# The first chunk's h in two 256-row halves, w1 in 256-column pieces, and a warm-up of 32-column tiles

## The chip, the cores and the metric

The kernel runs on one core of one Trainium2 chip. The metric is device time in microseconds (us). Every timed execution quoted here is fast, with a granted TensorE clock of 0.999 to 1.0. The profile of a kernel is one execution, and its span is about 1.8 us shorter than its device time. PE is TensorE, DVE VectorE, ACT ScalarE, SPq the queue of transfers that SyncE issues.

## The reference

A dense layer with SiLU, forward and backward, in bfloat16: x is 2048 x 640, w1 640 x 1536, w2 1536 x 640. The kernel returns the output and the three gradients.

```python
h = silu(einsum("bsd,df->bsf", x, w1))
out = einsum("bsf,fd->bsd", h, w2)
# returned: out, and the gradients of x, w1 and w2 for a given grad_out
```

## The kernel before

It works in four chunks of 512 rows. For a chunk it makes h transposed (w1's columns on the partitions), then the out phase (h times w2). The first chunk decides the ramp: it needs x transposed (xT), which PE makes from x in its natural layout, and w1. Warm-up matmuls on zeros keep PE busy until x is there.

```python
NWARM = 36
warm = cpool.tile([P, P], dt_in, name="warm")
nc.vector.memset(warm[:], 0.0)
for i in range(NWARM):
    nc.tensor.matmul(wp[:, 0:P], lhsT=warm[:], rhs=warm[:], start=True, stop=True)
# ... (cut)
nc.sync.dma_start(out=x_nat[:, 0:STC, :], in_=x_v[:, 0:STC, :])          # 512 rows, 640 KB
nc.sync.dma_start(out=w1_nat[:, :, 0:FH], in_=w1_v[:, :, 0:FH])          # 256 columns, 320 KB
nc.sync.dma_start(out=w1_nat[:, :, FH:FC], in_=w1_v[:, :, FH:FC])        # 320 KB
for fc in range(1, NFC):                                                 # 2 x 640 KB
    nc.sync.dma_start(out=w1_nat[:, :, fc * FC:(fc + 1) * FC], in_=...)
for hf in range(2):                                                      # w2, halves of its columns
    nc.sync.dma_start(out=w2_nat[:, :, hf * DH:(hf + 1) * DH], in_=...)
goT_next = load_goT(0)                                                   # a transposing load
# ... (cut: transposing loads of w2 and w1)
xT_next = pe_xT(0, 1)                     # 20 PE transposes, copies by DVE and ACT

def h_group(ft, xT, aT, ghT):             # 128 columns of h: 5 matmuls of 512 columns
    hp = ps_h.tile([P, SC], FP32, name="hp")
    for dt_ in range(DT):
        nc.tensor.matmul(hp[:], lhsT=w1_nat[:, dt_, ft * P:(ft + 1) * P], rhs=xT[:, dt_, :], ...)
    # ... (cut: SiLU and its derivative on ACT and DVE)

def sd_phase(...):                        # the out phase
    for ft in range(FT):
        for hf in range(2):               # the second matmul already reads w2's second half of columns
            nc.tensor.matmul(op_[:, hf, 0:DH], lhsT=lhs_all[:, ft, ...],
                             rhs=rhs_all[:, ft, hf * DH:(hf + 1) * DH], ...)
```

## Time and profile before

| | before |
|---|---|
| device time, median of 3 | 323.03 us (323.01 to 323.51) |
| span of the profile | 321.2 us |
| x landed, first h matmul | 5.01 us, 6.35 us |
| first out-phase matmul | 19.30 us |
| the two parts of w2 landed | 14.79 us and 18.60 us |

The head of the page: busy time of PE, and its digits over 40 slices of 8 us.

```profile
PE 316.2 (98%) x1926; PEld 188.5 (59%) x1944; DVE 99.1 (31%) x172; ACT 78.9 (25%) x136; POOL 0.7 (0%) x6
...
PE   8999999999999999999999999999999999999996
...
PEclk9999999999999999999999999999999999999999
...
PE 97%; DMA 1%; issue 0%; DVE 0%; DVEq 0%
```

PE is never idle for long after the first slice, and the chain of waits that ended last (the last line) is PE itself. So the kernel can only get shorter where PE has nothing to do, at the start. The table of PE's waits shows all there is:

```profile
PE wp L90 <- DVE warm L85: 1.0, 1, 1.0
PE tp L118 <- DMA x_nat<-in_x_dram: 0.3, 1, 0.3
```

The timeline of PE, first 20 us (start, duration, line, operation; in brackets the idle time before and what ended it):

```profile
0.99 3.81 PE L90 MATMUL wp<-warm 128*128 128x128 bf16 x36 [0.99 <-DVE warm L85]
5.06 1.30 PE L118 MATMUL tp<-ident,x_nat 128*128 128x128 bf16 x20 [0.26 <-DMA x_nat<-in_x_dram]
6.35 13.11 PE L144 MATMUL hp<-xT,w_nat 128*128 128x512 bf16 x58
19.30 0.98 PE L180 MATMUL op<-w_nat,aT 128*128 128x320 bf16 x6
```

The warm-up covers the wait for x. Its matmuls start 107 ns apart up to 4.38 us and 56 ns apart from 4.47: the array's clock opens there. The page's row PEclk does not show this, it has 9 throughout. x lands, is transposed, and from 6.35 us PE works through. (Two of the 60 h matmuls have no record.) The same start in the chain of waits:

```profile
0.74 4.26 DMA x_nat<-in_x_dram
5.01 0.05 issue
5.06 1.30 PE tp L118 x20
6.35 0.37 PE hp L144
```

### The profile page before, as it was taken

The page shows a single profiled execution, that of the slowest core. Times are in us where ns is not written, and L with a number is a line of the kernel's source. Part 1 is how long each engine was busy: PE and PEld are TensorE (multiplying, and loading weights), DVE is VectorE, ACT ScalarE, POOL GpSimd, SP SyncE. Part 2 cuts the span into 40 slices and gives each one's busy share as a digit, 9 for nine tenths or more (in the row PEclk, how much of TensorE's full clock was granted, in tenths as well). Part 3 has the DMA queues.
Part 4 walks back from the last instruction along what each step waited for, and adds up shares of the span by engine and source line. Part 5 has one row for each costly group of instructions (what it writes and reads, how often), then busy time and mean ns, then how long its engine had stood idle before and what let it go on. Part 6 is the DMA issues. An engine that isn't in the chain of part 4 may idle for free.

```text
span 321.2 us, 4386 instructions
## 1 busy us (share of the span) xinstructions
PE 316.2 (98%) x1926; PEld 188.5 (59%) x1944; DVE 99.1 (31%) x172; ACT 78.9 (25%) x136; POOL 0.7 (0%) x6
## 2 busy tenths in 40 slices
PE   8999999999999999999999999999999999999996
PEld 6467457544577644477754467777777775444443
DVE  1860553577501287800357740220000000110001
ACT  3961000455210155411044521001111111000100
POOL 0000000000000000000000000000000000000000
PEclk9999999999999999999999999999999999999999
DMA  7999999998794020291020079909999996211111
GB/s 235 318 191 200 220 274 241 363 289 274 213 290 137 6 78 0 78 316 67 17 82 0 0 254 245 239 17 236 226 218 213 266 219 211 85 38 44 35 42 41
DMA packets 113731, 52.32 MB, mean 163 GB/s; under 512 B 84144, under 2 KB 113712, under 8 KB 113712
## 3 DMA queue, kind: packets, MB, share of 16 engines
q1 hardware_dynamic: 113712, 52.04, 64.1%
q8 instruction: 15, 0.25, 0.3%
q14 instruction: 4, 0.03, 0.0%
HBM read 9.18 MB, written 21.76 MB: 96 GB/s over the span
## 4 chain that ended last, share of the span: by engine, by line
PE 97%; DMA 1%; issue 0%; DVE 0%; DVEq 0%
PE op L180 32%; PE op L263 16%; PE hp L163 16%; PE hp L144 16%; PE hp L302 15%; DMA x_nat<-in_x_dram 1%; PE hp L284 1%; PE tp L118 0%; DVE g_2755 L295 0%; DVEq L295 0%
## 5 line engine op out<-in xcount | busy, mean ns | idle before, releaser
L144 PE MATMUL hp<-xT,w_nat 128*128 128x512 bf16 x229 | 56.3, 379 | 0.6
L163 PE MATMUL hp<-goT,w2T 128*128 128x512 bf16 x238 | 56.8, 379 | 0.1
L180 PE MATMUL op<-w1T,ghT 128*128 128x320 bf16 x384 | 52.8, 299 | 0.0
L180 PE MATMUL op<-w_nat,aT 128*128 128x320 bf16 x384 | 52.8, 299 | 0.0
L263 PE MATMUL op<-go_nat,a_blk 128*128 128x320 bf16 x384 | 52.3, 299 | 0.0
L151 ACT ACTIVATE aT<-hp 128x512 bf16<-128x512 f32 x48 | 28.7, 597 | 83.0 <-PE hp L144 83.0
L302 PE MATMUL hp<-gh_blk,x_nat 128*128 128x512 bf16 x219 | 48.2, 379 | 0.3
L180 PEld LDWEIGHTS <-aT 128*128 128x128 bf16 x384 | 37.5, 98 | 15.3
L180 PEld LDWEIGHTS <-ghT 128*128 128x128 bf16 x384 | 37.5, 98 | 14.8
L263 PEld LDWEIGHTS <-a_blk 128*128 128x128 bf16 x384 | 37.5, 98 | 14.7
L163 PEld LDWEIGHTS <-w2T 128*128 128x128 bf16 x240 | 23.5, 98 | 28.2
L144 PEld LDWEIGHTS <-w_nat 128*128 128x128 bf16 x240 | 23.4, 98 | 27.8
L170 DVE SCALAR_TENSOR_TENSOR ghT<-ghT,hp 128x512 bf16<-128x512 bf16 x48 | 32.5, 682 | 16.2 <-PE hp L163 16.2
L191 DVE CAST o_sb<-op 128x640 bf16<-128x640 f32 x16 | 13.2, 825 | 78.6 <-PE op L180 78.6
L302 PEld LDWEIGHTS <-x_nat 128*128 128x128 bf16 x224 | 21.9, 98 | 26.3
L156 DVE SCALAR_TENSOR_TENSOR ghT<-aT,v 128x512 bf16<-128x512 bf16 x48 | 33.0, 687 | 0.6
L153 ACT ACTIVATE t<-hp 128x512 f32<-128x512 f32 x48 | 28.4, 592 | 0.0
L155 DVE TENSOR_SCALAR v<-t 128x512 bf16<-128x512 f32 x48 | 20.5, 427 | 20.5 <-ACT t L153 20.5
L189 ACT ACTIVATE o_sb<-op 128x640 bf16<-128x640 f32 x16 | 11.2, 703 | 49.1 <-PE op L180 49.1
L270 ACT ACTIVATE gw_sb<-op 128x640 bf16<-128x640 f32 x12 | 8.4, 704 | 56.8 <-PE op L263 56.8
L313 DVE CAST g_2475<-hp 128x512 bf16<-128x512 f32 x1 | 0.7, 690 | 58.2 <-PE hp L302 58.2
L90 PE MATMUL wp<-warm 128*128 128x128 bf16 x36 | 3.8, 304 | 1.0 <-DVE warm L85 1.0
(31 smaller groups left out, 26.2 us busy)
## 6 DMA issues: line engine op xcount, KB each, us to landing
aT_scr<-aT SPq DMA_DIRECT2D x4, 1536.0 KB, 6.3
ghT_scr<-ghT SPq DMA_DIRECT2D x4, 1536.0 KB, 9.6
out_dram<-o_sb SPq DMA_DIRECT2D x8, 640.0 KB, 4.4
x_nat<-in_x_dram SPq DMA_DIRECT2D x4, 640.0 KB, 5.4
go_nat<-in_grad_out_dram SPq DMA_DIRECT2D x4, 640.0 KB, 7.0
w_nat<-in_w_dram SPq DMA_DIRECT2D x2, 960.0 KB, 11.5
out_dram<-gw_sb SPq DMA_DIRECT2D x1, 1920.0 KB, 6.9
w_nat<-in_w_dram SPq DMA_DIRECT2D x2, 640.0 KB, 7.6
```

The costliest lines, as they stand in the source:

```text
L144: nc.tensor.matmul(hp[:], lhsT=w1_nat[:, dt_, ft * P:(ft + 1) * P], rhs=xT[:, dt_, :], start=(dt_ == 0), stop=(dt_ == DT - 1),)
L151: nc.scalar.activation(aT[:, ft, :], hp[:], ACT.Silu)
L153: nc.scalar.activation(t[:], hp[:], ACT.Tanh, scale=0.5)
L155: nc.vector.tensor_scalar(out=v[:], in0=t[:], scalar1=-0.5, scalar2=0.5, op0=ALU.mult, op1=ALU.add)
L156: nc.vector.scalar_tensor_tensor(out=ghT[:, ft, :], in0=aT[:, ft, :], scalar=1.0, in1=v[:], op0=ALU.subtract, op1=ALU.mult)
L163: nc.tensor.matmul(gp[:], lhsT=w2T[:, dt_, ft * P:(ft + 1) * P], rhs=goT[:, dt_, :], start=(dt_ == 0), stop=(dt_ == DT - 1),)
L170: nc.vector.scalar_tensor_tensor(out=ghT[:, ft, :], in0=ghT[:, ft, :], scalar=1.0, in1=gp[:], op0=ALU.add, op1=ALU.mult)
L180: nc.tensor.matmul(op_[:, hf, 0:DH], lhsT=lhs_all[:, ft, sl * P:(sl + 1) * P], rhs=rhs_all[:, ft, hf * DH:(hf + 1) * DH], start=(ft == 0), ...
L189: nc.scalar.activation(dst, op_[:, :, 0:DH], ACT.Copy)
L191: nc.vector.tensor_copy(out=dst, in_=op_[:, :, 0:DH])
L263: nc.tensor.matmul(op_[:, hf, 0:DH], lhsT=a_blk[:, st, :], rhs=go_nat[:, st, hf * DH:(hf + 1) * DH], start=(st == 0), stop=(st == ST - 1),)
L302: nc.tensor.matmul(gp[:], lhsT=x_nat[:, st, dt_ * P:(dt_ + 1) * P], rhs=gh_blk[:, st, :], start=(st == 0), stop=(st == ST - 1),)
```

## The change

Its intent is to start h sooner. Only 256 rows of x (320 KB, on two issuing queues) come ahead of w1 and are transposed by PE; the other 256 come as a transposing load behind w1. h of the first chunk is made for one half of the rows and then for the other, two blocks of 128 columns in one PSUM tile (a buffer that PE writes its sums to), each pair with its own 320 KB piece of w1. The warm-up is shorter, 25 groups of four matmuls, each on 32 columns of the array, and four full matmuls more.

```diff
-    NWARM = 36
+    NWARM = 25
+    NFILL = 4
@@
         for i in range(NWARM):
-            nc.tensor.matmul(wp[:, 0:P], lhsT=warm[:], rhs=warm[:], start=True, stop=True)
+            for q in range(0, P, 32):
+                nc.tensor.matmul(
+                    wp[q:q + 32, 0:P], lhsT=warm[:, 0:32], rhs=warm[:], start=True, stop=True
+                )
@@
-        nc.sync.dma_start(out=x_nat[:, 0:STC, :], in_=x_v[:, 0:STC, :])
-        (w1 in pieces of 256, 256, 512 and 512 columns)
+        nc.sync.dma_start(out=x_nat[:, 0, :], in_=x_v[:, 0, :])
+        nc.scalar.dma_start(out=x_nat[:, 1, :], in_=x_v[:, 1, :])
+        for fp in range(F // XH):
+            nc.sync.dma_start(
+                out=w1_nat[:, :, fp * XH:(fp + 1) * XH], in_=w1_v[:, :, fp * XH:(fp + 1) * XH]
+            )
+        nc.sync.dma_start_transpose(out=xT_next[:, :, XH:SC], in_=x2[XH:SC, :])
         (w2, goT, w2T, w1T as before)
@@
-        xT_next = pe_xT(0, 1)
+        (per 128 rows 5 transposes; DVE copies blocks 0 to 2, ACT blocks 3 and 4)
+        for i in range(NFILL):
+            nc.tensor.matmul(wp[:, 0:P], lhsT=warm[:], rhs=warm[:], start=True, stop=True)
@@
+        def h_pair(ft, half, xT, aT, ghT):
+            lo, hi = half * XH, (half + 1) * XH
+            hp = ps_h.tile([P, SC], FP32, name="hp")
+            for g in range(2):
+                h_mm(hp[:, g * XH:(g + 1) * XH], ft + g, xT, lo, hi)
+            h_tail(...)
@@
             if c == 0:
-                for ft in range(FT):
-                    h_group(ft, xT, aT, ghT)
+                for half in range(2):
+                    for ft in range(0, FT, 2):
+                        h_pair(ft, half, xT, aT, ghT)
```

(The lines in brackets stand for cut parts, and dots for cut arguments. Rows 256 to 511 of x in their natural layout are needed only at the end, and now come in chunk 2. Left out too: ACT's first use of SiLU, which loads its table, moves behind the issue of the loads.)

More of the change, by code (lines that the diff above doesn't have):

```diff
@@ L86 @@
         warm_a = cpool.tile([P, 1], FP32, name="warm_a")
-        nc.scalar.activation(warm_a[:], warm[:, 0:1], ACT.Silu)
         wp = ps_h.tile([P, SC], FP32, name="wp", tag="hp")
         for i in range(NWARM):
-            nc.tensor.matmul(wp[:, 0:P], lhsT=warm[:], rhs=warm[:], start=True, stop=True)
+            for q in range(0, P, 32):
+                nc.tensor.matmul(
+                    wp[q:q + 32, 0:P], lhsT=warm[:, 0:32], rhs=warm[:], start=True, stop=True
+                )
         ident = cpool.tile([P, P], dt_in, name="ident")
@@ L108, in load_goT @@
             return goT
-        def pe_xT(c, halves):
-            xT = xpool.tile([P, DT, SC], dt_in, name="xT")
-            nst = STC // halves
-            for hh in range(halves):
-                for dt_ in range(DT):
-                    tp = ps_h.tile([P, nst, P], dt_in, name="tp", tag="hp")
-                    for j in range(nst):
-                        st = c * STC + hh * nst + j
-                        nc.tensor.transpose(tp[:, j, :], x_nat[:, st, dt_ * P:(dt_ + 1) * P], ident[:])
-                    dst = xT[:, dt_, hh * nst * P:(hh + 1) * nst * P]
-                    if dt_ % 2 == 0:
-                        nc.vector.tensor_copy(out=dst, in_=tp[:].rearrange("p j q -> p (j q)"))
-                    else:
-                        nc.scalar.copy(out=dst, in_=tp[:].rearrange("p j q -> p (j q)"))
-            return xT
-        FH = FC // 2
-        nc.sync.dma_start(out=x_nat[:, 0:STC, :], in_=x_v[:, 0:STC, :])
-        nc.sync.dma_start(out=w1_nat[:, :, 0:FH], in_=w1_v[:, :, 0:FH])
-        nc.sync.dma_start(out=w1_nat[:, :, FH:FC], in_=w1_v[:, :, FH:FC])
-        for fc in range(1, NFC):
-            nc.sync.dma_start(out=w1_nat[:, :, fc * FC:(fc + 1) * FC], in_=w1_v[:, :, fc * FC:(fc + 1) * FC])
+        XH = SC // 2
+        NXH = XH // P
+        xT_next = xpool.tile([P, DT, SC], dt_in, name="xT")
+        nc.sync.dma_start(out=x_nat[:, 0, :], in_=x_v[:, 0, :])
[4 more added lines that the diff above has]
+            )
+        nc.scalar.activation(warm_a[:], warm[:, 0:1], ACT.Silu)
+        nc.sync.dma_start_transpose(out=xT_next[:, :, XH:SC], in_=x2[XH:SC, :])
         for hf in range(2):
@@ L137, with h_tail, h_mm @@
         nc.sync.dma_start_transpose(out=w1T[:], in_=w1[:, :])
-        xT_next = pe_xT(0, 1)
-        def h_group(ft, xT, aT, ghT):
-            hp = ps_h.tile([P, SC], FP32, name="hp")
+        DS = 3
+        for st in range(NXH):
+            tp = ps_o.tile([P, 2, 8, P], dt_in, name="tp", tag="op")
+            for dt_ in range(DT):
+                b, q = (0, dt_) if dt_ < DS else (1, dt_ - DS)
+                nc.tensor.transpose(tp[:, b, q, :], x_nat[:, st, dt_ * P:(dt_ + 1) * P], ident[:])
+            nc.vector.tensor_copy(out=xT_next[:, 0:DS, st * P:(st + 1) * P], in_=tp[:, 0, 0:DS, :])
+            nc.scalar.copy(out=xT_next[:, DS:DT, st * P:(st + 1) * P], in_=tp[:, 1, 0:DT - DS, :])
+        for i in range(NFILL):
+            nc.tensor.matmul(wp[:, 0:P], lhsT=warm[:], rhs=warm[:], start=True, stop=True)
+        def h_tail(hp, a_out, gh_out):
+            nc.scalar.activation(a_out, hp, ACT.Silu)
+            t = tpool.tile([P, SC], FP32, name="t")
+            nc.scalar.activation(t[:], hp, ACT.Tanh, scale=0.5)
+            v = tpool.tile([P, SC], dt_in, name="v")
+            nc.vector.tensor_scalar(out=v[:], in0=t[:], scalar1=-0.5, scalar2=0.5, op0=ALU.mult, op1=ALU.add)
+            vv = v[:] if len(a_out.shape) == 2 else v[:].rearrange("p (g s) -> p g s", g=a_out.shape[1])
+            nc.vector.scalar_tensor_tensor(
+                out=gh_out, in0=a_out, scalar=1.0, in1=vv, op0=ALU.subtract, op1=ALU.mult
+            )
+        def h_mm(hp, ft, xT, lo, hi):
             for dt_ in range(DT):
                 nc.tensor.matmul(
-                    hp[:],
+                    hp,
                     lhsT=w1_nat[:, dt_, ft * P:(ft + 1) * P],
-                    rhs=xT[:, dt_, :],
+                    rhs=xT[:, dt_, lo:hi],
                     start=(dt_ == 0),
@@ L150, in h_group @@
                 )
-            nc.scalar.activation(aT[:, ft, :], hp[:], ACT.Silu)
-            t = tpool.tile([P, SC], FP32, name="t")
-            nc.scalar.activation(t[:], hp[:], ACT.Tanh, scale=0.5)
-            v = tpool.tile([P, SC], dt_in, name="v")
-            nc.vector.tensor_scalar(out=v[:], in0=t[:], scalar1=-0.5, scalar2=0.5, op0=ALU.mult, op1=ALU.add)
-            nc.vector.scalar_tensor_tensor(
-                out=ghT[:, ft, :], in0=aT[:, ft, :], scalar=1.0, in1=v[:], op0=ALU.subtract, op1=ALU.mult
-            )
+        def h_group(ft, xT, aT, ghT):
+            hp = ps_h.tile([P, SC], FP32, name="hp")
+            h_mm(hp[:], ft, xT, 0, SC)
+            h_tail(hp[:], aT[:, ft, :], ghT[:, ft, :])
+        def h_pair(ft, half, xT, aT, ghT):
+            lo, hi = half * XH, (half + 1) * XH
+            hp = ps_h.tile([P, SC], FP32, name="hp")
+            for g in range(2):
+                h_mm(hp[:, g * XH:(g + 1) * XH], ft + g, xT, lo, hi)
+            h_tail(hp[:].rearrange("p (g s) -> p g s", g=2), aT[:, ft:ft + 2, lo:hi], ghT[:, ft:ft + 2, lo:hi])
         def g_group(ft, goT, ghT):
@@ L205 @@
             if c == 2:
+                nc.sync.dma_start(out=x_nat[:, NXH:STC, :], in_=x_v[:, NXH:STC, :])
                 for j in range(STC, ST, STC):
```

## The prediction

> **What bounds the kernel.** TensorE. The page shows PE busy for 316.2 of 321.2 us, and the chain that ended last is 97% PE; its only waits are 1.0 us (memset) and 0.3 us (x). From 6.35 us, the first h matmul, PE runs without a gap. So only when h starts, and whether loads starve PE soon after, can move the time.
>
> **Start, before (timeline, chain).** 36 warm-up matmuls run from 0.99 to 4.8 us, 107 ns apart; from 4.47 us they come 55 ns apart, so the clock opens after 3.4 us of work (the Trainium skill, "TensorE: Matmul & The Clock Gate", Part 1, says the same). x (640 KB) lands at 5.0 us, 20 transposes take 1.30 us, the first w1 piece lands at 6.04, h starts at 6.35 and lasts 12.95 us (60 matmuls, 216 ns apart). The out phase starts at 19.30 us and its second matmul needs the second half of w2, which lands at 18.5 us: 0.8 us of slack.
>
> **What changes.**
> - Before h only 320 KB of x are needed. At 1.05 us per 320 KB x should be there at about 4.0 us; 10 transposes take about 0.65 us, the copies 0.4 us: h could start at 5.1 to 5.3 us, 1.1 us earlier.
> - Warm-up: 100 matmuls in 25 groups of four. If a group takes the 107 ns of one cold matmul (the skill, same page, Part 3: column tiles run concurrently), it ends at 3.7 us. Serial, it would end near 8 us (estimate: 107 ns to 4.4 us, 55 ns after).
> - h is 120 matmuls of 256 columns, estimate 109 ns: 13.1 us, +0.15.
> - A pair of column blocks takes 1.09 us and needs a new 320 KB piece, which takes 1.04 to 1.13 us to land: h now runs at the pace of the loads. In the instruction order the fourth h matmul already needs the second w1 piece (estimate 6.1 us), about 0.5 us of stall.
> - The other half of xT comes by a transposing load behind w1. Such loads move 290 GB/s with about 1 us of overhead each (3.3 us per 640 KB for w2T): 2.1 us after w1 has landed, about 12.3 to 13 us; needed at about 12.3. Stall 0 to 0.7 us.
> - w2 stands behind that load: about 1 us less x ahead of it, about 2 us of transposing more.
> - PE's instruction fetch (16 KB on one DMA engine, 1.1 us) came at 15.2 us, after 196 PE instructions, and held w2's last share. 200 warm-up instructions move it to about 3.5 to 5 us, among x and w1.
>
> **Sum.** 1.1 us gained at the first h matmul; 0.5 lost to w1, 0.1 to narrower matmuls, 0.3 to xT's half; and 0.4 (0 to 1.5) to w2 and the moved fetch. The out phase starts at about 19.5 us against 19.3. Everything after is the same PE work (later loads have microseconds of slack), so the change is about +0.2 us.
>
> **Prediction: 323.2 us, 8 in 10 between 321.9 and 324.8.** Faster by over 2%: 0.005; within 2%: 0.98; slower by over 2%: 0.015.
>
> **What would show it.** First transposes near 4 us; first h near 5.2 us; a PE wait on the second w1 piece about 0.3 us later; a wait on xT's second half; the first out-phase matmul between 18.5 and 20.5 us.
>
> **What would make it wrong.** Tiles that do not overlap (h near 9 us, +2.5 us); a clock that opens later, so that h starts at 216 ns per 256 columns (up to +3 us); loads that keep up everywhere (321.7 us); the moved fetch holding w1 for over 1 us (324.5 us).

## The result, and the profile after

| | before | after |
|---|---|---|
| device time, median of 4 and 4 | 323.27 us (323.01 to 323.70) | 323.37 us (323.19 to 323.59) |
| ratio of the fast runs | | 1.0002, 95% interval 0.9985 to 1.0019 |
| span of the profile | 321.2 us | 321.6 us |
| first h matmul | 6.35 us | 5.18 us |
| first out-phase matmul | 19.30 us | 19.67 us |

A ratio here is the mean time of one kernel's fast runs over the mean of the other's from the same rounds, so it is not quite the ratio of the medians quoted.

The page's head, PE's waits, and PE's timeline of the changed kernel:

```profile
PE 316.2 (98%) x2062; PEld 193.3 (60%) x2062; DVE 98.6 (31%) x171; ACT 78.5 (24%) x136; POOL 0.7 (0%) x6
...
PE   6999999999999999999999999999999999999996
...
PEclk9999999999999999999999999999999999999999
...
PE 97%; DMA 2%; SPq 0%; DVE 0%; issue 0%; DVEq 0%
```

```profile
PE hp L155 <- DMA w_nat<-in_w_dram: 1.2, 1, 1.2
PE wp L91 <- DVE warm L86: 1.0, 1, 1.0
PE hp L155 <- DVE xT L137: 0.4, 1, 0.4
```

```profile
0.99 2.86 PE L91 MATMUL wp<-warm 128*32 128x128 bf16 x100 [0.99 <-DVE warm L86]
3.78 0.40 PE L140 MATMUL wp<-warm 128*128 128x128 bf16 x4
4.01 0.72 PE L136 MATMUL tp<-ident,x_nat 128*128 128x128 bf16 x10
5.18 0.49 PE L155 MATMUL hp<-xT,w_nat 128*128 128x256 bf16 x3 [0.45 <-DVE xT L137]
6.89 12.95 PE L155 MATMUL hp<-xT,w_nat 128*128 128x256 bf16 x117 [1.22 <-DMA w_nat<-in_w_dram]
19.67 1.11 PE L195 MATMUL op<-w_nat,aT 128*128 128x320 bf16 x7
```

The intended gain is there: h starts 1.17 us sooner. Three matmuls later PE stops, because the fourth needs the second piece of w1. The chain of waits now runs through that load, where before it ran through x:

```profile
1.68 5.17 DMA w_nat<-in_w_dram
6.84 0.05 issue
6.89 12.95 PE hp L155 x117
```

The sum, from the start times of the matmuls: first h matmul 6.349 to 5.182, -1.17 us. The third h matmul starts at 5.399 and the fourth at 6.891 where 0.109 later would be usual: +1.38. 120 matmuls of 256 columns, 109 ns apart, for 60 of 512, 216 ns apart: +0.15. Together +0.37; the out phase moved by 19.674 - 19.297 = +0.38, and the span by 0.4.

Nothing after that differs. Span less the start of the second out-phase matmul (the first that can wait for w2's second part) is 301.8 us in the kernel before and in the kernel after, and it is 301.8 to 302.0 in all twelve experiments. (With the 1.8 us between span and device time, a run without a profile can be estimated to have started its second out-phase matmul at its time less 303.6 us.)

Why was the second piece late? A load gives sixteen landing events. The Trainium skill, "DMA: Bandwidth & Descriptors", section "Why a DMA increments its semaphore by 16 and not by 1", says that each DMA engine that takes part adds one when its share is in, and that only all sixteen mean that the data are there. For the second piece the trace has them at 5.40 us (first), 5.76 (ninth) and 6.84 (last). In the kernel before, the load that ends after the same 960 KB has 5.41, 5.88 and 6.08. So half of the engines were sooner than before, and the last was 0.76 us later. Two things are visible at that time. In the stretch from 4.0 to 5.4 us the engines were not all busy. Each line has the stretch, its length, the busy time of PE, PEld, DVE, ACT and POOL, the granted clock, the DMA engines' mean busy share (over 1 where the times of an engine's packets overlap), and GB/s; first the kernel before, then after:

```profile
4.00:5.40 1.40, 1.14 (x16) 0.97 (x15) 0.00 (x0) 0.00 (x0) 0.00 (x0) 1.00 1.11 331
```

```profile
4.00:5.40 1.40, 0.95 (x17) 0.85 (x13) 0.64 (x2) 0.52 (x2) 0.00 (x0) 1.00 0.94 272
```

And at 5.62 us one packet of 16,384 bytes on the instruction queue took 885 ns. From the queue view of the changed kernel, 5 to 7 us (queue, packets, MB, share of the sixteen engines):

```profile
q1 hardware_dynamic: 1207, 0.60, 106.7%
q8 instruction: 1, 0.02, 2.8%
```

In the kernel before, the first such packet came at 15.18 us, when 196 PE instructions had been recorded, and the next ones after another 252 and 247. The 200 warm-up instructions (each matmul has a weight load) bring it into w1. The trace does not name the owner of this queue; that the packets are PE's instructions is read from their place, which moves with the number of PE instructions (e2, e8).

### The profile page after: what moved, and what is told of

Read it like the earlier page. It is cut to its first block, busy times and chain, and to the rows that moved or that the text cites. A ratio compares the mean times of both kernels' runs of the same rounds, so it can differ in the third digit from the quotient of the medians.

```text
span 321.6 us, 4645 instructions
## 1 busy us (share of the span) xinstructions
PE 316.2 (98%) x2062; PEld 193.3 (60%) x2062; DVE 98.6 (31%) x171; ACT 78.5 (24%) x136; POOL 0.7 (0%) x6
## 4 chain that ended last, share of the span: by engine, by line
PE 97%; DMA 2%; SPq 0%; DVE 0%; issue 0%; DVEq 0%
PE op L195 32%; PE op L280 16%; PE hp L155 16%; PE hp L178 16%; PE hp L319 15%; DMA w_nat<-in_w_dram 2%; PE hp L301 1%; SPq L119 0%; SPq L116 0%; DVE g_2874 L312 0%; DVEq L312 0%
## 5 line engine op out<-in xcount | busy, mean ns | idle before, releaser
L155 PE MATMUL hp<-xT,w_nat 128*128 128x512 bf16 (+1 forms) x300 | 57.2, 336 | 1.7 <-DMA w_nat<-in_w_dram 1.2
L155 PEld LDWEIGHTS <-w_nat 128*128 128x128 bf16 x300 | 29.3, 98 | 24.1 <-DMA w_nat<-in_w_dram 1.8
L147 DVE TENSOR_SCALAR v<-t 128x512 bf16<-128x512 f32 x48 | 20.5, 426 | 22.5 <-ACT t L145 22.5
L204 ACT ACTIVATE o_sb<-op 128x640 bf16<-128x640 f32 x16 | 11.3, 704 | 49.1 <-PE op L195 49.1
L91 PE MATMUL wp<-warm 128*32 128x128 bf16 x100 | 2.9, 313 | 1.0 <-DVE warm L86 1.0
```

The source lines that it names most:

```text
L147: nc.vector.tensor_scalar(out=v[:], in0=t[:], scalar1=-0.5, scalar2=0.5, op0=ALU.mult, op1=ALU.add)
L155: nc.tensor.matmul(hp, lhsT=w1_nat[:, dt_, ft * P:(ft + 1) * P], rhs=xT[:, dt_, lo:hi], start=(dt_ == 0), stop=(dt_ == DT - 1),)
L204: nc.scalar.activation(dst, op_[:, :, 0:DH], ACT.Copy)
```

## The experiments

Twelve kernels ran, all with correct results. A piece is called in, or complete, at the last of its sixteen landing events. In the table, out is the start of the second out-phase matmul in the profiled run, and times are medians. Ratios are to the kernel before in the same rounds, where its medians were 323.19 (e1 to e4), 323.09 (e5 to e8) and 323.28 us (e9 to e12). By a measure of 2% every kernel here is as fast as the one before; the differences discussed are of 0.1 to 0.2%.

| run | first h | out | time | ratio (95%) |
|---|---|---|---|---|
| before | 6.35 | 19.43 | 323.27 | |
| after | 5.18 | 19.81 | 323.37 | 1.0002 (0.9985 to 1.0019) |
| e1 source order | 5.90 | 19.74 | 323.21 | 1.0001 (0.9989 to 1.0014) |
| e2 full warm-up | 5.78 | 19.68 | 323.79 | 1.0009 (0.9997 to 1.0021) |
| e3 order + full | 5.39 | 19.88 | 323.56 | 1.0011 (1.0000 to 1.0023) |
| e4 before + tiles | 6.97 | 20.05 | 323.04 | 0.9995 (0.9982 to 1.0008) |
| e5 order + full + w2 rows | 5.30 | 18.99 | 322.58 | 0.9983 (0.9969 to 0.9997) |
| e6 after + w2 rows | 5.90 | 19.53 | 323.29 | 1.0000 (0.9987 to 1.0012) |
| e7 before + w2 rows | 6.81 | 19.89 | 323.38 | 1.0003 (0.9990 to 1.0016) |
| e8 e5, wide warm-up | 6.00 | 19.30 | 323.49 | 1.0000 (0.9987 to 1.0013) |
| e9 e5, x on one queue | 5.64 | 18.95 | 322.66 | 0.9981 (0.9969 to 0.9993) |
| e10 e5, w1 in four pieces | 5.78 | 19.90 | 323.80 | 1.0018 (1.0005 to 1.0030) |
| e11 e5, tiles again | 5.90 | 19.36 | 323.35 | 1.0006 (0.9993 to 1.0020) |
| e12 e9 + e10 | 5.96 | 20.34 | 323.92 | 1.0016 (1.0004 to 1.0028) |

### e1: h matmuls in source order

The scheduler had put the second pair's first matmul fourth, ahead of those that wait for ACT's copy of xT. The experiment chains the matmuls of the first half in source order on PE, without a wait, so that the second piece of w1 is needed by the eleventh.

```diff
+                if chain:   # half 0 only
+                    if prev:
+                        tc.add_manual_dep(mm.ins, prev[-1].name, <no wait, order only>)
+                    prev.append(mm.ins)
```

> Changed kernel, but the h matmuls of the first 256 rows are held in source order, so PE needs the second w1 piece at its 11th h matmul instead of its 4th. Theory A (the order costs the time): first h stays at 5.2 us, the piece still lands at about 6.85, the PE wait shrinks from 1.38 us to about 0.6, the out phase starts 0.5 to 0.75 us earlier, unless the second half of xT (12.46 us) or w2's second part (19.2 us) then ends a new wait; time about 322.8. Theory B (the loads pace h whatever the order, a wait saved at the second piece returns at the third to sixth): PE waits on the later pieces, out phase within 0.2 us of 19.67, time unchanged at 323.3.

Measured: 323.21 us, ratio 1.0001. The wait at the second piece is gone in this profile, partly because the first h matmul came only at 5.90: the TensorE clock had not opened when the transposes ran (they came 107 ns apart instead of 56). A wait on the third piece took its place (last landing 8.60 us):

```profile
4.17 1.27 PE L136 MATMUL tp<-ident,x_nat 128*128 128x128 bf16 x10
5.90 2.46 PE L157 MATMUL hp<-xT,w_nat 128*128 128x256 bf16 x20 [0.45 <-DVE xT L137]
8.65 1.05 PE L157 MATMUL hp<-xT,w_nat 128*128 128x256 bf16 x8 [0.28 <-DMA w_nat<-in_w_dram]
```

The late clock makes this profile a poor test of the wait at the second piece, but not of the wait at the third: that piece was in at 8.60 us, and the 100 matmuls behind it, 109 ns apart, end at 19.6 us however early h began. The six times, none below 323.10, are what Theory B said: the order chooses which piece PE waits for. Theory A falls as a cause by itself.

### e2: full warm-up matmuls

```diff
-            for q in range(0, P, 32):
-                nc.tensor.matmul(wp[q:q + 32, 0:P], lhsT=warm[:, 0:32], rhs=warm[:], ...)
+            nc.tensor.matmul(wp[:, 0:P], lhsT=warm[:], rhs=warm[:], ...)
```

> Changed kernel with 25 full 128-column warm-up matmuls in place of 100 tiles: 150 PE instructions fewer ahead of h. Theory A (PE's instruction fetch at 5.62 us is what holds the second w1 piece): the fetch moves to about 12 us, the second piece lands at 5.9 to 6.1 us, the PE wait shrinks from 1.38 to about 0.5 us; w2 now meets the fetch. Theory B (the piece is late because of the loads themselves, 512-byte rows and a dip of the queue at 4.0 to 5.4 us): it still lands at 6.5 us or later. Clock: if the tiles open it earlier, it now opens near 4.4 us as in the kernel before, so that the transposes start at 107 ns each and h starts 0.3 to 0.5 us later; if the moment is a matter of the window's phase, it may be 3.8 us here too.

Measured: 323.79 us, ratio 1.0009. The fetch moved to 13.11 us, the second piece was in at 6.13, close to the 5.9 to 6.1 us of Theory A, and h ran without a stop and ended 0.73 us sooner than in the changed kernel. But the next limit was there already. The out phase's second matmul waited for the second part of w2, which landed at 19.64:

```profile
18.95 0.30 PE L192 MATMUL op<-w_nat,aT 128*128 128x320 bf16 x1
19.68 1.52 PE L192 MATMUL op<-w_nat,aT 128*128 128x320 bf16 x10 [0.44 <-DMA w_nat<-in_w_dram]
```

The profiled execution (323.30) was one of this kernel's two fast ones; three others took 323.8 to 324.1 (estimate: second out-phase matmul at 20.2 to 20.5 us), and what they met has no trace. The first h matmul came at 5.78 us, because the clock opened only after the transposes, later than the 4.4 us expected.

The fetch now hit the first part of w2: fifteen of its landing events are at 15.38 us or before, the last at 16.89. The second part came late with it. From w1's last piece to w2's second part it took 8.9 us in e2 and in e3, but 7.9 and 7.7 us in the changed kernel and in e1, whose fetch is in w1. So the full warm-up did not take the fetch away from the loads, it moved it from w1 to w2, where it costs about 1.0 us; by these landing times that is as long as the waits for w2 in e2 (0.60) and e3 (0.98) or longer. No run without a fetch in either load tests this.

### e3: both

> Both edits together. If order and fetch are separate causes the PE waits among the first 20 h matmuls sum to under 0.2 us, and the next limit shows: the second half of xT or the second part of w2 at the start of the out phase (about 19 us). Time 322.5 to 323.0. If it is no faster than the better of the two alone, they are one cause, or w2's landing has become the bound.

Measured: 323.56 us, ratio 1.0011. h waits for w1 once, for 0.1 us (second piece in at 6.61), ends at 18.77 us, half a microsecond before that of the kernel before, and PE then waits for w2 even longer than in e2:

```profile
PE wp L90 <- DVE warm L86: 1.0, 1, 1.0
PE op L202 <- DMA w_nat<-in_w_dram: 0.8, 1, 0.8
PE hp L154 <- DVE xT L134: 0.4, 1, 0.4
```

The expected 322.5 to 323.0 was missed; the second half of the expectation, that w2 would become the bound, is what came.

### e4: the tiled warm-up in the kernel before

> Kernel before with only the warm-up changed: 36 groups of four 32-column tiles, 216 more PE instructions. If tiles overlap, warm-up still ends near 4.8 us or earlier. Theory A (the moved fetch hurts the loads it meets): the fetch comes near 4 us, x or the first w1 piece lands 0.6 to 1.1 us later than 5.01 and 6.08, h starts near 7.0 instead of 6.35, time +0.5 to +1.0 us. Theory B (fetch harmless): h starts at 6.35, time unchanged. Clock: if tiles open it earlier, the 56 ns pace shows before 4.0 us instead of 4.4.

(The edit is the reverse of e2's, in the kernel before: 36 groups of four.)

Measured: 323.04 us, ratio 0.9995. The fetch came at 6.55 us, later than expected and after x. (323 PE instructions had been recorded by then, 195 to 249 in the other thirteen profiles, so the count alone does not give its moment.) It met the third load of w1: fifteen events at 9.34 us or before, the last at 10.57. That load is needed only at the fifth group of h (estimate 6.97 + 4 x 1.08 = 11.3 us), so nobody waited. This late share cost nothing, because its load had slack; the time is what Theory B said. h did start at 6.97, the number of Theory A, but not for its reason: x and the first piece landed 0.25 and 0.28 us later than in the kernel before, both before the fetch, and the clock opened late. It opened at 6.13 us in this profile, so 4 x 32 columns did not open it sooner.

### e5: source order, full warm-up, and w2 in blocks of rows

The out phase walks w2 row block by row block, so with w2 loaded as two blocks of rows it can begin with the first 960 KB.

```diff
         for hf in range(2):
-            nc.sync.dma_start(out=w2_nat[:, :, hf * DH:(hf + 1) * DH], in_=...)
+            fs = slice(hf * FT // 2, (hf + 1) * FT // 2)
+            nc.sync.dma_start(out=w2_nat[:, fs, :], in_=w2_v[:, fs, :])
```

> Source order, full warm-up matmuls, and w2 loaded as two blocks of rows instead of two halves of columns, so that the out phase needs only the first 960 KB to begin and the second 1.6 us later. Theory A (after the w1 wait is gone, w2's last share is the only bound left; in the two profiles without the early fetch h ended at 18.95 and 18.77 us and the out phase waited 0.74 and 1.12 us for w2): no wait at the out phase, which starts at 18.7 to 19.0 us; time 0.5 to 0.9 us below the changed kernel, 322.4 to 322.8. Theory B (some further wait, xT's half or w1's last piece, takes its place): out phase at 19.4 or later, 323.2 as ever.

Measured: 322.58 us, ratio 0.9983, interval below 1. h stops once, 0.29 us, before its eleventh matmul, and the out phase follows h without a wait, at 18.85 us:

```profile
17.76 1.25 PE L155 MATMUL hp<-xT,w_nat 128*128 128x256 bf16 x10
18.85 2.34 PE L203 MATMUL op<-w_nat,aT 128*128 128x320 bf16 x16
```

Theory A holds. This beats the kernel before by 0.5 us of 323, and by the medians the changed kernel too (322.58 against 323.37, from different rounds; e6, the changed kernel with w2's blocks of rows alone, took 323.29 in the same rounds as e5). e9 below, which is e5 with one issue moved, repeats the gain in other rounds.

### e6 and e7: the blocks of rows alone

Only the edit of w2 above, in the changed kernel (e6) and in the kernel before (e7).

> Changed kernel with only w2's blocks of rows. Its out phase did not wait for w2 (19.23 us landed, 19.81 needed), so if the w1 wait is its whole loss nothing moves: out phase near 19.67, time 323.3 within 0.2 us. If w2 costs it something in unprofiled executions, up to 0.3 us less.

> Kernel before with only w2's blocks of rows. There w2 had 0.8 us of slack and the start is bound by x; nothing should move: out phase at 19.3 us, time 323.2 within 0.2 us. If it gains as much as the version with all three edits, that version owes its gain to w2 alone and not to the early start.

Measured: ratios 1.0000 and 1.0003. In both w2 was not what PE waited for, and the times did not move. (The out phases of the two profiles, 0.3 us before and 0.5 us after what was expected, carry a clock that opened late in both, which delayed h to 5.90 and 6.81 us; in e6 that also shortened the wait for the second piece, in at 6.42.) So w2's layout alone gains nothing (e6, e7), and neither does mending w1 alone (e2, e3): one limit was left each time, and e5 removes both.

### e8: a warm-up of 512-column matmuls

```diff
-    NWARM = 25
+    NWARM = 8
-            nc.tensor.matmul(wp[:, 0:P], lhsT=warm[:], rhs=warm[:], ...)
+            nc.tensor.matmul(wp[:], lhsT=warm[:], rhs=warm_w[:], ...)   # warm_w: 512 columns of zeros
```

> As the version with all three edits, but the warm-up is 8 matmuls of 512 columns (34 PE instructions fewer, same 3.4 us): the instruction fetch moves to about 15 us, into w2's second block, which has 1.6 us of slack. If the fetch matters only through what it meets, the time is that of the version with all three edits or up to 0.2 us less; the warm-up ends near 4.4 us, so h may start 0.3 us later than 5.2.

Measured: 323.49 us, ratio 1.0000; the expected time was missed. The fetch moved to 15.99 us, near the 15 expected. The second memset delayed the warm-up to 1.26 us and it ended at about 4.8, so that h started 0.7 us later than in e5. The five runs fall into two groups, 322.59 and 322.92 against 323.49, 323.59 and 323.70; the profile is of the second of the fast ones, and what the others met is open.

### e9, e10, e12: the loads themselves

e9 issues both x tiles from the sync queue; e10 loads w1 as 256, 256, 512 and 512 columns; e12 has both. All stand on e5.

```diff
-        nc.scalar.dma_start(out=x_nat[:, 1, :], in_=x_v[:, 1, :])                      # e9, e12
+        nc.sync.dma_start(out=x_nat[:, 1, :], in_=x_v[:, 1, :])
-        for fp in range(F // XH):                                                      # e10, e12
+        for lo, hi in ((0, XH), (XH, FC), (FC, 2 * FC), (2 * FC, F)):
```

> The version with all three edits, with both x tiles issued from the sync queue. In four profiles without an early instruction fetch the last engine's share of the second w1 piece still landed at 6.13 to 6.71 us, three or four engines late, after a dip of the queue at 4.0 to 5.4 us. Theory A (two issuing queues upset the even spread over the engines): the dip goes, the second piece lands by 6.2. Theory B (it is the loads themselves): no change, 6.1 to 6.7 us. Time in either case within 0.3 us of 322.6.

Measured: 322.66 us, ratio 0.9981, second piece in at 6.31 us, the busy share from 4.0 to 5.4 us 1.04 at 294 GB/s. The dip is smaller and not gone, and the piece is in where Theory B said. The kernel is as fast as e5; which issuing queue takes the second x tile does not show in the time.

> The version with all three edits, with w1 in four pieces (256, 256, 512, 512 columns) as in the kernel before. If the 512-byte rows or the number of issues cause the dip, it shrinks, and w1 is in 0.3 to 0.6 us sooner (last piece before 10.6 us); the third pair waits for a 640 KB piece, at about 8.0 us, needed at 7.5: a PE wait of about 0.5 us. Time 322.5 to 323.0.

Measured: 323.80 us, ratio 1.0018. w1 was in 0.45 us sooner than in e5 (10.58 against 11.03), but the third pair of h waited for its 640 KB piece (8.79 us):

```profile
5.78 2.45 PE L153 MATMUL hp<-xT,w_nat 128*128 128x256 bf16 x20 [0.45 <-DVE xT L133]
8.84 1.38 PE L153 MATMUL hp<-xT,w_nat 128*128 128x256 bf16 x11 [0.61 <-DMA w_nat<-in_w_dram]
```

The wait was 0.78 us by start times, where 0.5 was expected, and the time missed its range by 0.8. The dip stayed as well (269 GB/s), so four issues for six did not mend it; the first two pieces kept their 512-byte rows. For a first chunk in halves the small pieces are the faster ones here: e9, with the small pieces, has 0.9981 in the same rounds.

> The version with all three edits, x on one queue and w1 in four pieces: the candidate for the fastest. If the two edits help apart, 322.3 to 322.6; otherwise as the worse of them. In every run the moment the clock opens (seen between 3.7 and 6.2 us) shifts the start by up to 0.7 us, so single runs spread by that much.

Measured: 323.92 us, ratio 1.0016: the same wait, 1.13 us long (piece in at 9.23), and a first h matmul at 5.96 because the first piece was in only at 5.91. The candidate for the fastest is among the slowest.

### e11: e5 with the tiled warm-up

> The version with all three edits, with the tiled warm-up put back: it differs from that version in the warm-up and in the place of the instruction fetch alone. Theory A (the early fetch costs): fetch at 5.5 to 5.9 us, one engine about 0.7 us later on the third to fifth w1 pieces, PE waits there, out phase near 19.4, time 323.0 to 323.3 against 322.6. Theory B (fetch hidden once order and w2 are mended): 322.6.

Measured: 323.35 us, ratio 1.0006, against 0.9983 for e5 in another set of rounds and 0.9981 for e9 in the same. The fetch came at 5.97 us as expected, and the third to fifth pieces were 0.3 us later than in e5 (8.17, 9.30 and 10.32 against 7.84, 8.97 and 10.05), where 0.7 was expected. In the profiled run (322.96, the fastest of six) PE did not wait for them, because the clock opened only after 6 us, which held the start at 5.90 and slowed the first h matmuls. So the tiled warm-up is about 0.2% slower here, but the profile does not say how much of that is the fetch and how much the clock; this stays open.

### What the fetch does to w1, over eight runs

The runs of the 256-column pieces with h's first half in whatever order, split by the place of the fetch. Last landing event, us:

| fetch | run | piece 2 | piece 3, ninth event | piece 3, last |
|---|---|---|---|---|
| 5.62 | after | 6.84 | 6.82 | 8.21 |
| 5.83 | e1 | 7.05 | 6.77 | 8.60 |
| 5.49 | e6 | 6.42 | 6.94 | 8.38 |
| 5.97 | e11 | 7.11 | 6.83 | 8.17 |
| 13.11 | e2 | 6.13 | 6.87 | 7.45 |
| 13.40 | e3 | 6.61 | 6.81 | 7.74 |
| 12.94 | e5 | 6.71 | 6.73 | 7.84 |
| 15.99 | e8 | 6.38 | 6.92 | 7.52 |

(e9, whose x came another way, has its fetch at 13.44 and 6.31, 7.19 and 7.58 in the other columns.) With the fetch in w1 the third piece is complete at 8.34 us on average, without it at 7.64, while the ninth of the sixteen events does not move (6.84 and 6.83). So the fetch delays the last share by 0.7 us and not the first nine. The two halves of the table differ in the warm-up too; that it is the fetch is seen where it moves: the late share goes with it, to w2's first part in e2 (fifteen events at 15.38 us, the last at 16.89) and to the third load of w1 in e4.

At the second piece the means are 6.86 and 6.46, with single runs that overlap: there the fetch is at most part of the lateness. The other part came without any fetch (6.1 to 6.7 us against 6.08 in the kernel before), together with the dip from 4.0 to 5.4 us. That dip was in e1 to e3, e5, e6 and e8 to e11 too (259 to 294 GB/s, against 331 to 351 in the runs of the kernel before, e4 and e7), and not in e12 (322), whose queue had a deeper one before, from 3.0 to 3.6 us. The 512-byte rows by themselves are not the cause: in the changed kernel the same rows went at 345 GB/s and a share of 1.14 from 3.3 to 3.9 us, just before the dip. What is the cause is not settled.

## Why the prediction was right

The time, 323.2 predicted and 323.37 measured, and the shift of the out phase, +0.2 against +0.38 us, came out within the range. The range of 2.9 us is wide, though: it holds the case that the prediction named as worst for the fetch (324.5), and misses the one without any stall (321.7) by only 0.2. So the time alone says little, and the terms have to be looked at one by one:

- **"1.1 us gained at the first h matmul": right.** 1.17 us. The first transposes started at 4.01 us and the first h matmul at 5.18, as foreseen. In part this was luck: in this profile the clock was open before the transposes. In e1, e6 and e11, with the same warm-up, it opened later and h started at 5.90. (The kernel before loses as well when the clock is late: 6.81 in e7.)
- **Tiles that overlap: right.** A group of four took 107 ns, the time of one full matmul of the same clock; the warm-up ended at about 3.8 us. The Trainium skill, "TensorE: Matmul & The Clock Gate", Part 3, says that column tiles run concurrently, and this trace agrees: the four start within 10 ns of each other.
- **"0.5 lost to w1": right in place, wrong in size.** PE did stop at the fourth h matmul for the second piece. The wait was 1.38 us, because the piece was complete at 6.84 us and not at 6.1. The estimate took the mean rate of the queue for the time of the last share. The moved fetch, which the prediction had foreseen among x and w1, may be about half of the difference (0.4 us by the means of the table above, whose single runs overlap); the rest came without a fetch, along with the dip, and is open.
- **"0.1 to narrower matmuls": right.** 0.15 us.
- **"0.3 to xT's half" and "0.4 to w2": did not come, because the longer wait at w1 covered them.** xT's half landed at 12.46 us, as estimated, but was needed only at 13.12. With the predicted 0.5 us at w1 it would have been needed 0.88 us sooner, at 12.24, and would have cost about 0.3, as predicted (estimates from these landing times). w2's second part landed at 19.23 us and was needed at 19.81. That w2 is a limit too is shown by e2 and e3, where it takes over as soon as w1 lets go, for 0.60 and 0.98 us (start times 0.737 and 1.118 apart, where 0.136 is usual); but there the fetch had moved into w2 and made it later by about 1.0 us. So the stalls lie one behind the other, and a longer one in front shortens those behind it. The prediction's w1 term was 0.9 too small, and the two terms behind it, 0.7 together, then came out as nothing. That the sum was near is this compensation, and not foresight.

So the gain of 1.17 us went into a wait on the second piece of w1, and behind that wait stood others that would have taken nearly all of it anyway: w2's second part, in at 19.23 us, would have let the second out-phase matmul start at about 19.28 (estimate), 0.15 sooner than the 19.43 of the kernel before.

## What to carry to other kernels

A ramp has several loads that end one after the other. Draw up for each when it lands and when it is needed, before moving the first: here mending the order (e1), the warm-up (e2), both (e3) or w2's layout (e6) gained nothing, and all three together gained 0.17% over the kernel before. Look at the last of a load's sixteen shares and not at the mean rate, and count the instructions that a change puts ahead of the critical loads, for their own fetch is a transfer too. A consumer that walks a tensor by rows can start sooner when it comes in blocks of rows; that gained only once the load was what PE waited for (e5, not e6 or e7).

## What the Trainium skill lacked or had wrong

- "TensorE: Matmul & The Clock Gate", Part 1 says that the window which opens the clock is free-running, and gives a spread of 500 ns to either side. (It also says that one kernel showed 6, 11 or 14 slow matmuls in different runs.) That the moment moves with no change of the program agrees with such a window, but the spread was larger. With PE busy from 0.99 us, the 56 ns pace began at 4.47 us in the kernel before and at 6.21 us in e7, whose PE work up to there is the same; in the changed kernel it began at 3.85 us, 2.9 us after PE's first matmul, sooner than the 3.4 us of work that the prediction took from the same Part. Over all fourteen profiles the opening lies between 3.8 and 6.4 us, and for the ramp that decided whether h could start at 5.2 or at 5.9 us.

```profile
5.10 1.78 PE L118 MATMUL tp<-ident,x_nat 128*128 128x128 bf16 x20
6.81 1.45 PE L145 MATMUL hp<-xT,w_nat 128*128 128x512 bf16 x6
```

  (The timeline of e7; the same 20 transposes took 1.30 us in the kernel before.)
- The same page, Part 4, says that the open clock does not engage for PE transposes and gives about 275 ns for one in context. Here they came 55 to 56 ns apart with the open clock (recorded at 215 to 230 ns each in the kernel before) and 107 ns apart without it (up to 314 ns each in e7), and in e7 the clock opened in the middle of them.
- The same page, Part 3, gives speedups of tiles for 512-column matmuls, 2.38 times for three column tiles. For 128 columns with the clock not yet open, four column tiles ran in the 107 ns that one full matmul of 128 columns takes.
- "Runtime: NRT & Kernel Launch" has a section on the fetch of instructions, but neither it nor any other page that was found tells what the fetch does to data loads: one packet of 16,384 bytes per 213 to 278 recorded PE instructions in the kernel before, 0.9 to 1.4 us long, and the last of sixteen shares of a load that it meets late by 0.7 us (w1's third piece) to 1.5 us (w2's first part in e2).
- "DMA: Bandwidth & Descriptors" has a section on transposing loads, but not how the plain load ahead of them lands: the sixth piece of w1, just ahead of xT's transposing load, landed on all sixteen engines between 11.24 and 11.32 us, while the fifth was spread from 8.59 to 10.36. In the kernel before, where plain loads follow, w1's last piece was spread from 10.32 to 11.21. Why is not shown.
